# Eleven weight casts and five casts of h on GpSimd in the first sixteen steps of an attention and MLP kernel

## Chip, cores and metric

The kernel runs on one core of one Trainium2 chip. The metric is device time in microseconds (us) of one execution, the lower the better. Engines: PE is TensorE (PEld its weight loads), DVE is VectorE, ACT is ScalarE, POOL is GpSimd, SP is SyncE, which issues most transfers.

## The reference, cut to what matters

```python
def _attn_ref(q, k, v):                       # (8, 8, 576, 64) each, window of 128
    scores = scale * q @ k.T + bias           # bias = -slope(head) * distance
    scores = where(0 <= distance < 128, scores, -1e9)
    attn = exp(scores - max(scores)); attn = attn / (sum(attn) + 1e-9)
    return attn @ v

x = attention output as (4608, 512)
h = maximum(x @ w_in, 0.0)                    # w_in (512, 2048)
out = (h * h) @ w_out                         # w_out (2048, 512)
```

All numbers are float32.

## The kernel before, in words

The 4608 tokens are cut into `NCH` = 9 chunks `c` of 512 tokens. For each chunk the attention output `x` is built for `NP` = 4 pairs of heads `p`, and the two products with the weights run over `NF` = 16 steps `f`, each with 128 of the 2048 middle columns. To keep float32 accuracy on TensorE, each operand is split into a high half (a cast to fp32r) and a low half (what the cast left), and each product is made of three: high by high, high by low, low by high. So `gemm1(c, f)` is 12 products of 128x128 by 128x512 into the one bank `g` (line 194), and `gemm2(c, f)` is 12 products into four banks `acc` (line 223).

Weights come in once, as pairs of 32-bit words in `raw[f]` (two transfers of 512 KB a step, line 159), and `convert(f)` turns them in five instructions of 128x1024: a Prelu on ScalarE (line 165), a shift on VectorE (167), a shift with an or on VectorE (169), the cast of the high half `wh` (171) and the subtraction on VectorE that gives the low half `wl` (173). In the planner these are `("c", f, 0)` to `("c", f, 4)`. The cast is on GpSimd for f in `CASTS`, on ScalarE otherwise.

Between the two products of a step stand four instructions of 128x512, `("h1", f, 0)` to `("h1", f, 3)`: the relu out of bank `g` on ScalarE (204), the square (for chunk 0 on ScalarE at line 209, on VectorE at line 207 for f in `SQUARES`), the cast `hh` on ScalarE (211) and the subtraction `hl` on VectorE (213).

Attention for chunk 0 is done in eight wide segments `k` = 0 to 7 (two a pair of heads), with steps named by letters: `s` scores (TensorE, line 508), `u` the largest score (VectorE, 518), `e` exp (ScalarE, 525), `r` the sum's reciprocal (VectorE, 258 and 259), `n` the normalisation (GpSimd at line 537, VectorE at 535 for k in `NORMS`), `z` transposes (TensorE, 544 and 547), `o` and `m` copies out of their banks (`o` at line 277 on ScalarE, on VectorE for k in `COPIES`; `m` at 551 on VectorE), `x` the values (TensorE, 291, into the bank that the planner calls `xa`), `h` the cast of the high half (ScalarE, 301) and `l` the subtraction for the low half (VectorE, 304), which frees `xa`. Chunks from 1 on are done in couples `q` from 4 on: scores (392), copies on ScalarE (419, 426, the planner's `base`), folds on VectorE (438, 442), then the same softmax in segments (244, 251, 258, 262), a transpose on VectorE (313), a way through DRAM (317, 322), two selects on GpSimd (326) and the values (338).

Everything up to the end of chunk 0's sixteen steps is put in order by `start(K)`. It adds steps to a `Plan` with an engine, a cost in us, the steps that must come before, a due time and the buffers taken and given back; `NUDGE` shifts single due times. `Plan.run` then goes through a list schedule: of the steps that can begin within 0.1 us (or `WAIT` times a step's cost) of the earliest, on its engine, the one due first is issued. What comes out is the order of instructions on each engine (PE, DVE, Activation, Pool, SP); on the chip each engine follows its own order and waits for semaphores. `Plan.shares` tells which steps of GpSimd and VectorE the planner keeps apart in time. A weight's steps may begin after the steps that `HOLD(f)` names: `('n', 3)` is the normalisation of segment 3, `('z', 7)` the transposes of segment 7.

The order that TensorE follows in the chunk's start: `g1a` (the first nine products of `gemm1(0, 0)`, after `("x", 7)` and `("l", 0)` to `("l", 5)`), the rest of it, `gemm1(0, 1)`, `gemm1(0, 2)`, `gemm2(0, 0)`, `gemm1(0, 3)`, and so on in turns, with scores and values of the couples in between. From chunk 1 on a plain loop gives the order on TensorE, and a scheduler orders the other engines.

Of the kernel before, what the change touches and what calls it, by code (L numbers as in the profile page):

```python
# [25 lines left out]
NSEG = 2 * NP * NCH  # L26
PER = S // 64
HEAT = 16
HOLD = lambda f: (('n', 3),) if f < 1 else (('n', 6),) if f < 2 else (('z', 7),)
WAIT = 0.1  # L30
HAND = {"SP": 2.0, "PE": 0.25}
PORT = ('t', 'c', 'h1')
CONVERT = (('Activation', 1.2), ('DVE', 0.7), ('DVE', 1.2), ('Activation', 1.15), ('DVE', 1.2))
# [3 lines left out]
SOON = (("z", 7),)  # L37
FIRST = 39
APART = lambda i, f, b: i == 0 and f % 4 == 0 and b < 2
CASTS = (0, 2, 15,)  # L40
COPIES = (3,)
SQUARES = (6,)
NORMS = (7,)
NUDGE = {
# [6 lines left out]
}  # L51
SYNC = mybir.DependencyInfo(mybir.DependencyClass.Sync, mybir.DependencyReason.DATA)
ORDER = mybir.DependencyInfo(mybir.DependencyClass.NoSync, mybir.DependencyReason.DATA)
# [8 lines left out]
class Kern:  # L62
# [98 lines left out]
    def convert(self, f):  # L161
# [8 lines left out]
        yield  # L170
        (nc.gpsimd.tensor_copy if f in CASTS else nc.scalar.copy)(wh, flo)
        yield
# [13 lines left out]
    def gemm1(self, c, f):  # L186
        nc = self.nc
        xs = [self.x[c, p] for p in range(NP)]
        g = self.g1.tile([128, 512], F32, name="g")
        i = 0  # L190
        for cc in range(NCC):
            wl, wh = self.block(0, f, cc)
            for w, part in ((wh, 0), (wh, 1), (wl, 0)):
                nc.tensor.matmul(g, w, xs[cc][:, part], start=i == 0, stop=i == 11)  # L194
                i += 1
                if (c, f, i) == (0, 0, 9):
                    yield
        yield
        r = self.hp.tile([128, 512], F32, name="r", bufs=1)
        hh = self.hp.tile([128, 512], F32R, name="hh")  # L200
        hl = self.hp.tile([128, 512], F32R, name="hl")
        self.h[c, f] = hh, hl
        with self.tc.high_priority(offset=100):
            self.relu = nc.scalar.activation(r, g, AF.Relu)  # L204
        yield
        if c or f in SQUARES:
            nc.vector.tensor_tensor(r, r, r, op=ALU.mult)  # L207
        else:
            nc.scalar.activation(r, r, AF.Square)
        yield  # L210
        nc.scalar.copy(hh, r)  # L211
        yield
        nc.vector.tensor_tensor(hl, r, hh.bitcast(F32), op=ALU.subtract)  # L213

# [18 lines left out]
class Segment:  # L233
# [42 lines left out]
    def out(self):  # L276
        (self.nc.vector.tensor_copy if self.k in COPIES else self.nc.scalar.copy)(self.own, self.z)

# [209 lines left out]
class Wide(Segment):  # L488
# [40 lines left out]
    def norm(self):  # L529
        for i in (0, 1) if self.skip else (None,):  # L530
            m, a = (slice(None), 0) if i is None else (slice(i, 4, 2), self.first[i])
            t, rec = self.t[:, m, a:256], self.nm[:, 8:12][:, m]
            if self.k in NORMS:
                for j in range(t.shape[1]):
# [23 lines left out]
class Plan:  # L558
# [7 lines left out]
        self.steps[name] = (engine, us, after, due + NUDGE.get(name, 0), do, rooms(take), rooms(free))  # L566

    def shares(self, name):
        return self.steps[name][0] == "Pool" or (name[0] in PORT and self.steps[name][0] == "DVE")

    def room(self, name, n):
        self.count[name] = [0.0] * n
# [1 line left out]
    def run(self):  # L574
        left, end, clock = dict(self.steps), {}, {"SP": 0.8}
        while left:
# [16 lines left out]
            on, span = self.steps[first[2]][:2]  # L593
            same = [r for r in ready if self.steps[r[2]][0] == on and r[0] <= first[0] + max(0.1, WAIT * span)]
            t, due, name = min(same, key=lambda r: (r[1], r[0]))
# [13 lines left out]
def start(K):  # L609
    P = Plan()  # L610
    for name, n in (("sc", 1), ("sa", 1), ("xa", 1), ("at", 1), ("zp", 1), ("tw", 4), ("t", 3), ("pp", 2), ("ld", 3), ("g", 1)):
        P.room(name, n)
    do = lambda fn, *a: lambda: fn(*a)
# [27 lines left out]
    for k in range(8):  # L641
        G = Wide(K, k)
        c, p, sg = G.c, G.p, G.sg
        n = lambda s, *m: (s, k, *m)
        after = [("q", c, p, 0), ("q", c, p, 1)][: sg + 1] + ([("s", k - 1)] if k else [])
        chain = lambda s: ((s, k - 1),) if k else ()
        d, slot, w = 4.0 * k, "sa" if k % 2 else "sc", 0.75 if G.skip else 1.0
        P.add(n("s"), "PE", 0.9 * w, tuple(after), d, G.scores, slot)
        for m in range(4):
            P.add(n("u", m), "DVE", 0.35 * w, (n("u", m - 1) if m else n("s"), ("k", p)), d - 1.5, do(G.top, m), None if m else "tw", slot if m == 3 else None)  # L650
            P.add(n("e", m), "Activation", 0.48 * w, (n("u", m),) + ((n("e", m - 1),) if m else ()), d + 0.5, do(G.exp, m))
        P.add(n("r"), "DVE", 0.4, (n("e", 3),), d + 1, G.sums)
        P.add(n("n"), *(("DVE", 0.9 * w) if k in NORMS else ("Pool", 2.05 * w)), (n("r"),), d + 1, G.norm)
        P.add(n("z"), "PE", 0.9 * w, (n("n"),) + chain("z"), d - 3, G.turn, ("at", "zp", "pp"), "tw")
        P.add(n("o"), "DVE" if k in COPIES else "Activation", 0.6, (n("z"),), d - 2, G.out, None, "at")
        P.add(n("m"), "DVE", 0.62 if w == 1 else 0.36, (n("z"),), d + 1, G.also, None, "zp")
        P.add(n("x"), "PE", 1.0, (n("m"), n("o"), ("v", c, p)) + chain("x"), d + 4, G.values, "xa", "pp")
        P.add(n("h"), "Activation", 0.4, (n("x"),), d + 2, G.high)
        P.add(n("l"), "DVE", 0.36, (n("h"),), d + 2, G.low, None, "xa")
        if sg == 1:  # L660
            P.add(n("ld"), "free", 0.0, (n("x"),), d + 2, None, None, None if p == 3 else "ld")
    for q in range(4, 9):
# [7 lines left out]
        for s in (1, 0):  # L670
            G, k = C.both[s], 2 * q + s
            n = lambda s, *m: (s, k, *m)
# [18 lines left out]
    for f in range(NF):  # L691
        d, last = CONV(f), ("w", f)
        g = K.convert(f)
        for i, (engine, us) in enumerate(CONVERT):
            if i == 3 and f in CASTS:
                engine, us = "Pool", 1.5
            P.add(("c", f, i), engine, us, (last,) + HOLD(f), d, lambda g=g: next(g, None))
            last = ("c", f, i)

    last = ["wide", ("x", 7)] + [("l", k) for k in range(6)]  # L700
    for f in range(NF + 2):
        if f < NF:
            g = K.gemm1(0, f)
            step, n = lambda g=g: next(g, None), len(CONVERT) - 1
            if f == 0:
                P.add("g1a", "PE", 2.1, tuple(last) + (("c", f, n),), GO, step, "g")
                last = ["g1a", ("l", 6), ("l", 7)]
            P.add(("g1", f), "PE", 2.8 if f else 0.7, tuple(last) + (("c", f, n),), 500 if f else GO, step, "g" if f else None)
            for i, (engine, us) in enumerate((("Activation", 0.6), ("Activation", 0.65), ("Activation", 0.62), ("DVE", 0.78))):
                if i == 1 and f in SQUARES:  # L710
                    engine, us = "DVE", 0.75
                free = "g" if i == 0 else None
                P.add(("h1", f, i), engine, us, (("h1", f, i - 1) if i else ("g1", f),), -1, lambda g=g: next(g, None), None, free)
            last = [("g1", f)]
        if 1 < f < NF:
            P.add(("g2", f - 2), "PE", 2.8, (("g1", f), ("h1", f - 2, 3)), 500, do(K.gemm2, 0, f - 2))
            last.append(("g2", f - 2))
# [4 lines left out]
def tile_attn_moe(ctx: ExitStack, tc: tile.TileContext, *aps):  # L722
    K = Kern(ctx, tc, *aps)
    K.const()
    with tc.manual_schedule(engines={ENGINES["PE"]}):
        with tc.manual_schedule(engines={e for n, e in ENGINES.items() if n != "PE"}):
            start(K)
# [86 lines left out]
```

## Time and profile before

| what | us |
|---|---|
| median of 3 runs | 956.03 |
| lowest and highest | 955.96, 956.26 |
| the profiled execution's own time | 956.69 |
| its span, first to last instruction | 955.0 |
| TensorE matmul busy in the span | 946.8 (99%) |
| VectorE, ScalarE, GpSimd busy | 496.5, 417.6, 214.6 |

The span is what the trace covers; the rest of the execution's own time lies around it. A busy share over the whole span says little here, since the start and the long loop behind it have different limits: the start is read in stretches and in the order of time on each engine. A row of a timeline has the start, the duration, the engine, the line of the kernel, the operation, the tile written and the tile read with their shapes, and in brackets the idle time of the engine ahead of it with what ended that. Rows that follow each other with the same line are merged (x12). TensorE's granted clock was 1.00 in the whole span, its level of 2.4 GHz.

### The profile page before, as it was taken

To read this page: it belongs to the slowest core of one execution; us is meant where nothing else is said; L and a number is where in the kernel's file an instruction comes from. 1 tells how busy PE (TensorE), PEld (TensorE's weight loads), DVE (VectorE), ACT (ScalarE), POOL (GpSimd) and SP (SyncE) were. 2 spreads that over 40 slices of the span, in tenths; PEclk is the share of its full clock that TensorE was granted. 3 is DMA by queue.
4 is the path that set the end of the run, shared out by engine and by line. 5 is a ranking of instruction groups with operands and counts; after the bars stand their busy time and mean duration, and the time that the engine had idled before them with its cause. 6 is when DMAs were issued, how large, how long until landed. Compare 5 with 4: busy or idle time off the path is not lost.

```text
span 955.0 us, 17236 instructions
## 1 busy us (share of the span) xinstructions
PE 946.8 (99%) x6392; PEld 796.4 (83%) x6392; DVE 496.5 (52%) x1334; ACT 417.6 (44%) x1107; POOL 214.6 (22%) x254
## 2 busy tenths in 40 slices
PE   9899999999999999999999999999999999999998
PEld 5688888888888888888888888888888888888886
DVE  6998864445545455444544454455545444433222
ACT  7898743333444444434433343334344343332222
POOL 4123331222222222222222222221222212220000
PEclk9999999999999999999999999999999999999999
DMA  9974423322433333222433232333322231111001
GB/s 349 404 274 151 146 67 119 83 64 68 124 84 83 84 88 107 72 77 73 127 84 83 77 108 71 83 83 96 114 74 71 71 95 45 45 45 45 1 1 44
DMA packets 72883, 95.10 MB, mean 100 GB/s; under 512 B 8032, under 2 KB 41952, under 8 KB 72800
## 3 DMA queue, kind: packets, MB, share of 16 engines
q1 hardware_dynamic: 72368, 93.36, 32.9%
q8 instruction: 50, 0.82, 0.4%
q10 hardware_dynamic: 432, 0.66, 0.2%
q14 instruction: 33, 0.27, 0.1%
HBM read 67.76 MB, written 26.21 MB: 98 GB/s over the span
## 4 chain that ended last, share of the span: by engine, by line
PE 95%; DMA 4%; ACT 0%; issue 0%; DVE 0%; SPq 0%; DVEq 0%
PE acc L223 42%; PE g L194 42%; PE at L338 6%; PE s L392 3%; PE g L392 2%; DMA raw<-in_dram 2%; DMA wide<-in_dram 1%; DMA qk<-in_dram 1%; PE at L392 0%; ACT raw L165 0%; DVE raw L167 0%; ACT t L426 0%; ACT t L419 0%; ACT o L229 0%; DVE xu L304 0%
## 5 line engine op out<-in xcount | busy, mean ns | idle before, releaser
L194 PE MATMUL g<-xu,w 128*128 128x512 f32 x1728 | 423.3, 394 | 0.8 <-issue 0.8
L194 PEld LDWEIGHTS g<-xu,w 128*128 128x128 f32 x1728 | 344.1, 209 | 56.2 <-issue 1.5
L223 PE MATMUL acc<-hh,w 128*128 128x512 f32 x1152 | 386.2, 396 | 0.0
L223 PEld LDWEIGHTS acc<-hh,w 128*128 128x128 f32 x1152 | 223.9, 194 | 44.3 <-issue 0.7
L207 DVE TENSOR_TENSOR r<-r 128x512 f32<-128x512 f32 x129 | 103.0, 799 | 248.2 <-ACT r L204 246.9
L204 ACT ACTIVATE r<-g 128x512 f32<-128x512 f32 x144 | 85.9, 596 | 326.8 <-PE g L194 316.4
L223 PE MATMUL acc<-hl,w 128*128 128x512 f32 x576 | 226.8, 394 | 0.0
L326 POOL TENSOR_SCALAR_AFFINE_SELECT pp<-pp 128x512 f32<-128x512 f32 x128 | 107.1, 840 | 211.1 <-DMA pp<-way 162.2
L213 DVE TENSOR_TENSOR hl<-r,hh 128x512 fp32r<-128x512 f32 x144 | 108.6, 754 | 69.3 <-ACT hh L211 68.4
L262 POOL TENSOR_TENSOR t<-t,nm 128x512 f32<-128x512 f32 x64 | 82.0, 1281 | 263.9 <-DVE nm L259 145.9
L223 PEld LDWEIGHTS acc<-hl,w 128*128 128x128 f32 x576 | 112.0, 194 | 19.9
L251 ACT ACTIVATE t<-t,nm 128x128 f32<-128x128 f32 x256 | 100.1, 393 | 56.8 <-DVE nm L244 56.8
L211 ACT CAST hh<-r 128x512 fp32r<-128x512 f32 x144 | 89.1, 619 | 75.8 <-DVE r L207 74.2
L438 DVE COPY_PREDICATED t<-cst,s 64x256 f32<-64x256 int32 x100 | 44.5, 445 | 41.0 <-ACT t L426 22.4
L313 DVE STREAM_TRANSPOSE pp<-t 128x512 f32<-128x512 f32 x64 | 45.2, 707 | 38.0 <-POOL t L262 37.9
L338 PEld LDWEIGHTS at<-pp,v 128*64 128x64 f32 x1024 | 55.2, 137 | 11.2 <-issue 10.8
L338 PE MATMUL at<-pp,v 128*64 128x128 f32 x1024 | 63.0, 276 | 0.0
L244 DVE CUSTOM_DVE_ANT_0 t<-t,cst 128x128 f32<-128x128 f32 x256 | 59.0, 293 | 1.0
L251 ACT ACTIVATION_READ_ACCUMULATOR t<-t,nm 128x1 f32 x256 | 48.3, 189 | 0.0
L392 PE MATMUL s<-qk 64*64 64x64 f32 (+2 forms) x1168 | 47.5, 251 | 0.8 <-ACT raw L165 0.8
L392 PEld LDWEIGHTS s<-qk 64*64 64x64 f32 x1168 | 43.0, 133 | 1.0 <-ACT raw L165 1.0
L428 POOL MEMSET t<- 64x128 f32 (+1 forms) x44 | 10.0, 228 | 138.7 <-PE g L392 129.8
(63 smaller groups left out, 472.6 us busy)
## 6 DMA issues: line engine op xcount, KB each, us to landing
raw<-in_dram SPq DMA_DIRECT2D x32, 512.0 KB, 8.7
way<-pp SPq DMA_DIRECT2D x256, 64.0 KB, 1.8
pp<-way SPq DMA_DIRECT2D x64, 256.0 KB, 2.8
qk<-in_dram SPq DMA_DIRECT2D x32, 320.0 KB, 3.6
v<-in_dram SPq DMA_DIRECT2D x32, 320.0 KB, 3.0
qk<-in_dram SPq DMA_DIRECT2D x38, 256.0 KB, 4.2
out_dram<-o SPq DMA_DIRECT2D x35, 256.0 KB, 4.3
v<-in_dram SPq DMA_DIRECT2D x3, 256.0 KB, 4.9
```

The source lines that it names most:

```text
L194: nc.tensor.matmul(g, w, xs[cc][:, part], start=i == 0, stop=i == 11)
L204: self.relu = nc.scalar.activation(r, g, AF.Relu)
L207: nc.vector.tensor_tensor(r, r, r, op=ALU.mult)
L211: nc.scalar.copy(hh, r)
L213: nc.vector.tensor_tensor(hl, r, hh.bitcast(F32), op=ALU.subtract)
L223: nc.tensor.matmul(self.acc[m], w, h, start=(f == 0 and i == 0), stop=(f == NF - 1 and i == 2))
L244: self.nc.vector.tensor_tensor_reduce(self.t[:, m], self.t[:, m], self.K.nrel(2 * self.p + m // 2), -0.125, BIG, ALU.add, ALU.min, self.nm ...
L251: return self.nc.scalar.activation(self.t[:, m], self.t[:, m], AF.Exp, bias=nm[:, m : m + 1], scale=-1.0, accum_out=nm[:, 4 + m : 5 + m],)
L262: self.nc.gpsimd.tensor_tensor(self.t, self.t, self.nm[:, 8:12].unsqueeze(2).to_broadcast([128, 4, 128]), op=ALU.mult)
L326: nc.gpsimd.affine_select(to, self.own, pattern=[[-32 * sign, 4], [0, 4], [-sign, 32]], compare_op=op, fill=0.0, base=0, channel_multiplie ...
L338: self.nc.tensor.matmul(self.X[r, o : o + 128].rearrange("p (a c) -> p a c", a=4), v[:, 2 * sg + k, r], src[:, :, 2 * j + i], start=sg == ...
L392: mm = nc.tensor.matmul(to, qk[r, q0 : q0 + 64], qk[r, k0 : k0 + 64 * n], start=True, stop=True, skip_group_check=True,)
```

## The change

The high halves of eleven weights instead of three are cast on GpSimd (`CASTS`), and of `hh` those of f = 1, 4, 8, 9 and 13 in chunk 0 (`SPLITS`, new). One square more goes to VectorE (f = 4 and 8 instead of 6), the normalisation of segment 0 goes to VectorE beside that of segment 7, and the copies `o` of segments 2 and 4 instead of 3. The planner's costs of `e`, `o`, `h` and of GpSimd's cast are others, `HOLD` names segment steps one earlier for f from 1 on, `WAIT` is 0, `NUDGE` is another list, and `Plan.shares` returns False: GpSimd and VectorE are planned side by side.

```diff
-HOLD = lambda f: (('n', 3),) if f < 1 else (('n', 6),) if f < 2 else (('z', 7),)
-WAIT = 0.1
+HOLD = lambda f: (('n', 3),) if f < 1 else (('n', 5),) if f < 2 else (('z', 6),)
+WAIT = 0
@@
-CASTS = (0, 2, 15,)
-COPIES = (3,)
-SQUARES = (6,)
-NORMS = (7,)
+CASTS = (0, 1, 2, 3, 4, 7, 10, 12, 13, 14, 15,)
+COPIES = (2, 4,)
+SPLITS = (1, 4, 8, 9, 13,)
+SQUARES = (4, 8,)
+NORMS = (0, 7,)
 NUDGE = {
-    ('u', 1, 3): -17, ('r', 2): 96, ('r', 4): -63, ('l', 4): -29, ('u', 5, 3): 104.5, ('r', 5): -13.5,
...
+    ('w', 4): 194, ('w', 7): 41.5, ('m', 0): 8.5, ('o', 2): -4.5, ('u', 3, 3): 81.5, ('u', 4, 3): 181,
+    ('u', 5, 3): -382, ('u', 6, 0): -20, ('e', 6, 0): -60, ('t', 9, 1): 1.5, ('square', 8): 20, ('t', 11, 3): 11,
+    ('c', 0, 2): 4, ('c', 0, 4): 8, ('c', 6, 1): 1.5, ('c', 10, 1): 8.5,
 }
@@
-        nc.scalar.copy(hh, r)
+        (nc.gpsimd.tensor_copy if c == 0 and f in SPLITS else nc.scalar.copy)(hh, r)
@@
     def shares(self, name):
-        return self.steps[name][0] == "Pool" or (name[0] in PORT and self.steps[name][0] == "DVE")
+        return False
@@
-            P.add(n("e", m), "Activation", 0.48 * w, (n("u", m),) + ((n("e", m - 1),) if m else ()), d + 0.5, do(G.exp, m))
+            P.add(n("e", m), "Activation", 0.49 if w == 1 else 0.44, (n("u", m),) + ((n("e", m - 1),) if m else ()), d + 0.5, do(G.exp, m))
@@
-        P.add(n("o"), "DVE" if k in COPIES else "Activation", 0.6, (n("z"),), d - 2, G.out, None, "at")
+        P.add(n("o"), *(("DVE", 0.61) if k in COPIES else ("Activation", 0.48)), (n("z"),), d - 2, G.out, None, "at")
@@
-        P.add(n("h"), "Activation", 0.4, (n("x"),), d + 2, G.high)
+        P.add(n("h"), "Activation", 0.3, (n("x"),), d + 2, G.high)
@@
             if i == 3 and f in CASTS:
-                engine, us = "Pool", 1.5
+                engine, us = "Pool", 1.25
@@
+                if i == 2 and f in SPLITS:
+                    engine, us = "Pool", 0.7
```

## Rows read from the trace of the kernel before

**Rows 1.** Stretches: window, us, busy PE, PEld, DVE, ACT, POOL, clock, DMA, GB/s
```profile
7.00:37.20 30.20, 28.84 (x298) 19.05 (x294) 28.14 (x107) 26.52 (x83) 13.66 (x14) 1.00 1.04 399
37.20:49.70 12.50, 10.89 (x91) 8.81 (x89) 11.77 (x32) 11.49 (x29) 1.10 (x1) 1.00 1.03 406
49.70:70.00 20.30, 20.30 (x116) 17.13 (x115) 19.85 (x44) 19.67 (x33) 4.86 (x6) 1.00 0.73 268
37.20:130.80 93.60, 91.99 (x642) 76.83 (x641) 84.89 (x178) 75.47 (x161) 26.68 (x32) 1.00 0.60 203
```
**Rows 2.** Timeline of TensorE, 37 to 53 us: first products and gaps
```profile
37.22 3.18 PE L194 MATMUL g<-xu,w 128*128 128x512 f32 x12
...
41.57 0.34 PE L392 MATMUL s<-qk 64*64 64x192 f32 x1 [0.81 <-ACT raw L165]
...
42.93 3.09 PE L194 MATMUL g<-xu,w 128*128 128x512 f32 x12
46.82 3.04 PE L194 MATMUL g<-xu,w 128*128 128x512 f32 x12 [0.80 <-issue]
...
52.50 2.96 PE L194 MATMUL g<-xu,w 128*128 128x512 f32 x12
```
**Rows 3.** Timeline of VectorE, 29 to 51 us
```profile
29.07 1.09 DVE L258 TENSOR_SCALAR nm<-nm 128x4 f32<-128x4 f32 x1
...
30.41 1.14 DVE L535 TENSOR_SCALAR tw<-tw,nm 128x256 f32<-128x256 f32 x4
...
31.80 1.22 DVE L173 TENSOR_TENSOR w<-raw,w 128x1024 fp32r<-128x1024 f32 x1
32.93 0.42 DVE L304 TENSOR_TENSOR xu<-acc,xu 128x256 fp32r<-128x256 f32 x1
33.26 0.68 DVE L551 COPY pp<-acc 128x512 f32<-128x512 f32 x1
...
35.73 0.42 DVE L304 TENSOR_TENSOR xu<-acc,xu 128x256 fp32r<-128x256 f32 x1
...
39.41 1.36 DVE L438 COPY_PREDICATED t<-cst,s 64x256 f32<-64x256 int32 x3 [0.60 <-ACT t L426]
...
41.45 2.36 DVE L173 TENSOR_TENSOR w<-raw,w 128x1024 fp32r<-128x1024 f32 x2
...
49.04 0.69 DVE L213 TENSOR_TENSOR hl<-r,hh 128x512 fp32r<-128x512 f32 x1
49.65 1.22 DVE L173 TENSOR_TENSOR w<-raw,w 128x1024 fp32r<-128x1024 f32 x1
```
**Rows 4.** Timeline of ScalarE, 30 to 38 us
```profile
30.36 0.37 ACT L301 CAST xu<-acc 128x256 fp32r<-128x256 f32 x1 [0.48 <-PE acc L291]
...
34.33 0.37 ACT L301 CAST xu<-acc 128x256 fp32r<-128x256 f32 x1 [0.67 <-PE acc L291]
...
35.90 1.21 ACT L171 CAST w<-raw 128x1024 fp32r<-128x1024 f32 x1
...
37.61 0.60 ACT L419 COPY t<-at 128x512 f32<-128x512 f32 x1
```
**Rows 5.** Timeline of GpSimd: a cast, and the longest wait for a transfer
```profile
28.95 1.19 POOL L171 CAST w<-raw 128x1024 fp32r<-128x1024 f32 x1 [2.75 <-ACT tw L525]
...
72.43 1.52 POOL L326 TENSOR_SCALAR_AFFINE_SELECT pp<-pp 128x512 f32<-128x512 f32 x2 [8.27 <-DMA pp<-way]
```
**Rows 6.** Instructions grouped by line and shape, 37.2 to 130.8 us
```profile
L173 DVE TENSOR_TENSOR w<-raw,w 128x1024 fp32r<-128x1024 f32 x15 | 19.4, 1304 | 0.1
L171 ACT CAST w<-raw 128x1024 fp32r<-128x1024 f32 x12 | 13.6, 1143 | 3.4 <-DVE raw L169 3.4
L213 DVE TENSOR_TENSOR hl<-r,hh 128x512 fp32r<-128x512 f32 x15 | 11.9, 795 | 2.7 <-ACT hh L211 2.5
L211 ACT CAST hh<-r 128x512 fp32r<-128x512 f32 x15 | 9.3, 623 | 0.4
L171 POOL CAST w<-raw 128x1024 fp32r<-128x1024 f32 x2 | 2.2, 1104 | 6.6 <-DVE raw L169 3.4 <-ACT t L419 3.2
```

5 rows, old and new, of the table NUDGE are left out of this document.

## The prediction

> **What bounds the kernel now.** I read the busy times by stretch first, to find the stretch in which the end of the run is still open [rows 1]. TensorE (the first busy column) is full from 49.7 us on: it works 20.30 of 20.30 us up to 70 us, and between 37.2 and 130.8 us it works 91.99 of 93.60 us, while the part up to 49.7 us alone holds 10.89 of 12.50. So all of the 1.61 us that TensorE lacks between its first large product and the sixteenth lies ahead of 49.7 us. From there on the time is a fixed row of products; it ends earlier only if that row begins earlier or the gaps ahead of 49.7 us close, and later only if a new gap opens.
>
> Next I read TensorE's order of time around the gaps [rows 2]. The first large product (`g1`, step f=0) starts at 37.22 us. A gap of 0.81 us lies before 41.57, where the scores of couple 5 wait; the product of f=1 then starts at 42.93. Another gap of 0.80 us lies before the product of f=2 at 46.82, which has to wait until its bank `g` has been read. By 52.50 us, f=3, there are no gaps any more.
>
> Then I read what the other engines do just ahead of these starts. Between 7 and 37.2 us VectorE is busy 28.14 of 30.20 us and ScalarE 26.52; from 37.2 to 49.7 us 11.77 and 11.49 of 12.50; from 49.7 to 70 us 19.85 and 19.67 of 20.30. GpSimd has 13.66, 1.10 and 4.86 in the same three [rows 1]. So the start is a queue on VectorE and ScalarE, with GpSimd nearly free from 28 to 50 us, and this is what the change draws on. VectorE is the scarcer of the two.
>
> **The path to the first large product.** It stands behind the values of segment 7 in TensorE's order, and those behind `l` of segment 6, which frees the one bank `xa`. On VectorE I count three delays on that way [rows 3 to 5]. First, the sum `r` of segment 7 (line 258, four columns) begins at 29.07 us and ends at 30.16, just behind the end of GpSimd's cast of weight 0 (28.95 + 1.19 = 30.14): it has waited the cast out, and of its 1.09 us I count 0.9 as delay, an estimate that leaves 0.2 for its own work. Second, `l` of segment 5 starts at 32.93 although ScalarE had cast its `h` by 30.36 + 0.37; the last of what stands ahead of it is the subtraction for weight 0, 31.80 to 32.93: 1.13 us. Third, `l` of segment 6 starts at 35.73, although its `h` was ready at 34.33 + 0.37 = 34.70: 1.03 us behind integer work for weight 1. Together 3.1 us, all of it order.
>
> **The change part by part.** All of it is in `start`; the loop behind it isn't touched, and no transfer is added or taken away, though SP's list can be put out in another order.
>
> *Casts.* Eleven instead of three go to GpSimd, so eight more: at 1.10 us each [rows 6] 8.8 us more there, and 8 x 1.14 = 9.1 us less on ScalarE. *Blocks of h.* Five casts of 128x512 leave ScalarE, 5 x 0.62 = 3.1 us [rows 6]. The trace doesn't show that cast on GpSimd: half a 128x1024 cast is 0.55 us, a whole one 1.10; I take 0.62, since the tile has half the columns, and so 3.1 us. GpSimd gets 11.9 us more in all, in the 93.6 us in which it is busy for 26.68 [rows 1]: it has room. In its queue a cast can stand behind a select that awaits a transfer; the longest such wait is 8.27 us [rows 5]. What waits for the cast is the subtraction on VectorE and all behind that in VectorE's list.
>
> *Cast of weight 1.* It stands on ScalarE at 35.90 us for 1.21, ahead of the copies of couple 4's scores (37.61) [rows 4]. From these follow the folds on VectorE at 39.41, and behind the folds, in VectorE's list, the subtraction for weight 1 at 41.45 [rows 3], for which the product of f=1 waits until 42.93; the folds also free the bank that the scores of couple 5 go into, at 41.57 [rows 2]. (The row there names ScalarE's weight work as what came last; the folds, done when the subtraction starts at 41.45, lie as close, and it is their bank, so I follow them.) With that cast on GpSimd the copies can start up to 37.61 - 35.90 = 1.7 us earlier. Bounds 0 and -1.7; I take -0.9, a little over the gap of 0.81 us, since the values of segment 7, whose cast `h` comes in between, don't move with it.
>
> *Order around segments 5 to 7.* Weight 1 may now be turned from norm 5 on (norm 6 before), the others from the transposes of segment 6 on (7 before), and the planner's costs for `o`, `h` and `e` differ. The three delays above can go, or others can take their place: weight 0 stays with GpSimd and weight 1 joins it. Bounds -3.1 and +1.5 (the next point); I take half of the gain, -1.5.
>
> *Norm 0 and the copies `o`.* Norm 0 goes to VectorE, at most the 1.14 us that norm 7 takes there; of `o`, segments 2 and 4 go to VectorE and 3 leaves it, which adds one copy of about 0.68 [rows 3]. That is up to 1.8 us more on an engine with 2.1 us idle in that stretch, against a shorter way for segment 0. I take 0 and keep +1.5 (1.8 less the 0.3 us by which it idles early on anyway, an estimate) as the other end of the point above. *Squares.* Two instead of one on VectorE (+0.69 us, the undisturbed time of line 213, also 128x512): nothing on the path.
>
> *GpSimd beside VectorE.* The planner no longer keeps them apart, so more operations of VectorE will be held up as the sum at 29.07 was. Two kinds show what that costs now: line 173 takes 1.304 us in the mean and line 213 0.795 [rows 6], against 1.22 and 0.69 in single instructions with no GpSimd work beside them [rows 3]. Times 15 each this is 1.3 + 1.6 = 2.9 us, beside 26.68 us of GpSimd: 0.11 us for each. These two are 31.3 of VectorE's 84.89 us; for the others I double the rate, 0.2, an estimate. The added 11.9 us would so cost VectorE 1.3 to 2.4 us; the other end is that each of them holds it up, 11.9 us. I take 3, near the measured rate, with a little more because nothing plans around it. VectorE idles 93.60 - 84.89 = 8.7 us between 37.2 and 130.8 us, which covers this; where the cover fails it costs TensorE directly (second rival). I put it at 0 on the path, bounds 0 and +4.
>
> *What is late next.* The gap of 0.80 us before f=2 [rows 2] waits for the read of bank `g` behind product f=1, with no other product to put in between: it stays.
>
> Sum: -0.9 - 1.5 = -2.4 us. The profiled execution took 956.69 us, its span 955.0; the median of the runs is 956.03, 0.66 below the profiled one. I take the change off the median: 953.6.
>
> The Trainium skill, SBUF — State Buffer, section "Who interferes with whom", has a rule against this change: a VectorE instruction in a two-port mode, or with two inputs in SBUF, and a GpSimd instruction that reads SBUF exclude each other for the whole instruction, and the later one waits in full. The sum at 29.07, which ends within 0.02 us of GpSimd's cast, agrees with it. By that rule alone no overlap is free, and the sum goes towards the second rival.
>
> **The rivals.** *First: the start is no shorter, 955.9 (954.2 to 957.5).* VectorE carries the start and gets no lighter; ScalarE's relief only moves the waits. For it: VectorE idles only 0.73 us in the 12.5 us before 49.7, and norm 0 and one copy are added to it ahead of that. Against it: two of the three delays are pure order, and the wait at 41.57 leads back to a ScalarE cast that goes. This also holds the case in which the new lists come out nearly as the old ones.
>
> *Second: GpSimd holds VectorE up until TensorE runs dry, 959.0 (958 to 961).* The place is 49.7 to 70 us, where VectorE idles 0.45 us and ScalarE 0.63. The weight for f=3 is ready at 49.65 + 1.22 = 50.87 us and its product starts at 52.50 [rows 2, 3], a margin of 1.63 us. If the casts of weights 3, 4 and 7 and the blocks h of 1 and 4 come in here, GpSimd has 3 x 1.10 + 2 x 0.62 = 4.5 us more. Where over 0.45 + 1.63 = 2.1 us of it holds VectorE up, TensorE waits: 2.4 us at the most here, and by the same working a like amount once more where weights 10 to 14 are cast, less what VectorE can idle away there. I price it at 3 us and more than the gain at the start being lost: 959.0. For it: the overlap seen at 29.07 is complete. Against it: 0.2 us per us of GpSimd gives 0.9 us here, below the 2.1. A cast behind a select that waits up to 8.27 us for its transfer [rows 5] would end in the same place, by another way.
>
> **How the numbers follow.** A gain at the start that holds: 0.47; no net gain: 0.31; TensorE starved: 0.22. The measurement can tell about 0.2%, 1.9 us, from no change, so under 954.1 is faster and over 957.9 slower. The forecast is 953.6, and its own range goes from 951.2 (both terms at their ends, -1.7 and -3.1) to 954.1. For 8 in 10 the range must hold the first rival and much of the second. The lower end is 951.0, which is those ends and 0.2 us of the second gap; the upper end is 959.5. Faster 0.47, same 0.31, slower 0.22.
>
> **What would show it.** Right: the first large product at about 35.7 us instead of 37.22; product f=1 some 4.8 us behind it instead of 5.7; product f=3 near 50.1; TensorE full from about 47.3 us on. ScalarE should be some 12 us lighter between 37.2 and 130.8 us, GpSimd 12 us heavier, and VectorE 2 to 5 us heavier in the same work, all in longer instructions, of lines 173 and 213 among others. Wrong: a first product at 37 us or later; a gap on TensorE behind 50 us, with a subtraction of a weight (line 173) just ended in front of it; waits on GpSimd of lines 171 or 211 behind a select.

## The result and the profile after

The changed kernel takes 960.91 us (960.84 to 961.25) against 956.05 us for the kernel before, a ratio of 1.0051 with a 95% interval of 1.0040 to 1.0062: 4.9 us slower, where 2.4 us faster was forecast (medians of six runs each). The profiled execution took 960.86 us, its span 959.1.

The stretches of after answer to [rows 1]; columns: window, us, then busy us of PE, PEld, DVE, ACT and POOL, the granted clock, DMA share and GB/s.

```profile
7.00:37.20 30.20, 28.97 (x296) 20.50 (x298) 28.20 (x108) 26.39 (x85) 13.51 (x13) 1.00 1.04 399
37.20:49.70 12.50, 11.25 (x94) 9.01 (x94) 11.77 (x31) 10.52 (x24) 4.49 (x4) 1.00 1.03 406
49.70:70.00 20.30, 19.79 (x151) 16.05 (x150) 20.10 (x38) 15.01 (x32) 9.30 (x10) 1.00 0.71 238
37.20:130.80 93.60, 88.04 (x616) 71.70 (x616) 90.38 (x173) 60.10 (x140) 44.26 (x41) 1.00 0.57 195
```

Up to 49.7 us TensorE works a little more than before. Behind that, where it had been full, it now lacks time: 88.04 instead of 91.99 of the 93.6 us. ScalarE is 15.4 us lighter (12 forecast), VectorE 5.5 heavier, and GpSimd 17.6 heavier, though only some 12 us of work came to it. The stretch is fixed in time, and by its end TensorE has done less (616 against 642 instructions), so a comparison over the same work follows with the first experiment.

TensorE in the order of time (answers to [rows 2]) shows where:

```profile
35.39 3.63 PE L192 MATMUL g<-xu,w 128*128 128x512 f32 x12
...
40.19 3.06 PE L192 MATMUL g<-xu,w 128*128 128x512 f32 x12 [1.17 <-issue]
...
50.38 0.63 PE L192 MATMUL g<-xu,w 128*128 128x512 f32 x2
...
51.32 2.61 PE L192 MATMUL g<-xu,w 128*128 128x512 f32 x10 [0.31 <-DVE w L171]
...
57.39 2.73 PE L192 MATMUL g<-xu,w 128*128 128x512 f32 x10 [0.20 <-DVE w L171]
...
87.81 0.37 PE L390 MATMUL s<-qk 64*64 64x192 f32 x1 [0.77 <-DVE t L440]
...
100.39 0.74 PE L192 MATMUL g<-xu,w 128*128 128x512 f32 x2 [0.52 <-POOL w L169]
...
102.49 2.62 PE L192 MATMUL g<-xu,w 128*128 128x512 f32 x10 [1.36 <-DVE w L171]
...
115.04 0.37 PE L390 MATMUL s<-qk 64*64 64x192 f32 x1 [1.16 <-DVE t L440]
```

The first product starts at 35.39 us instead of 37.22 and that of f=3 at 50.38 instead of 52.50: the start is shorter. In the start one gap is left, 1.17 us ahead of f=1: ScalarE's relu out of bank `g` ends just before it, at 39.50 + 0.60 = 40.10 us, and the scores of couple 5, which stood there before, now come behind f=1. Then the product of f=3 stops after two of its twelve parts for the subtraction of its weight, and so does f=4. At 100.39 the product of f=10 waits for GpSimd's cast of its weight and again for the subtraction behind it; two sets of scores wait for folds on VectorE. The starts of products in the traces, in us:

| kernel | f=0 | f=1 | f=3 | f=8 | f=10 | f=11 | f=12 | chunk 1, f=0 |
|---|---|---|---|---|---|---|---|---|
| before | 37.22 | 42.93 | 52.50 | 84.07 | 98.91 | 104.51 | 111.69 | 138.54 |
| after | 35.39 | 40.19 | 50.38 | 83.48 | 100.39 | 107.75 | 116.51 | 143.42 |
| after, less before | -1.83 | -2.74 | -2.12 | -0.59 | +1.48 | +3.24 | +4.82 | +4.88 |

The whole difference is there when chunk 1 begins. All that was gained, and 4.8 us more, goes between f=3 and f=12: 1.5 us of it up to f=8, 5.4 from there on. The gaps in this stretch add up to 4.3 of these 6.9 us; the rest lies in rows that count as busy, 61.81 us from f=3 to f=12 for the same products that took 59.19 us before.

What holds the weight of f=10 up, first GpSimd in the order of time (answers to [rows 5]):

```profile
91.16 1.62 POOL L324 TENSOR_SCALAR_AFFINE_SELECT pp<-pp 128x512 f32<-128x512 f32 x1 [5.01 <-DVE nm L257]
92.73 0.61 POOL L209 CAST hh<-r 128x512 fp32r<-128x512 f32 x1
...
98.30 2.03 POOL L169 CAST w<-raw 128x1024 fp32r<-128x1024 f32 x1 [1.15 <-DVE raw L167]
100.26 1.11 POOL L209 CAST hh<-r 128x512 fp32r<-128x512 f32 x1
```

and VectorE in the same microseconds (answers to [rows 3]):

```profile
93.38 1.17 DVE L211 TENSOR_TENSOR hl<-r,hh 128x512 fp32r<-128x512 f32 x1 [1.18 <-POOL hh L209]
...
98.16 1.22 DVE L171 TENSOR_TENSOR w<-raw,w 128x1024 fp32r<-128x1024 f32 x1
99.30 1.60 DVE L165 TENSOR_SCALAR raw<-raw 128x1024 int32<-128x1024 int32 x1
100.81 1.63 DVE L171 TENSOR_TENSOR w<-raw,w 128x1024 fp32r<-128x1024 f32 x1
```

GpSimd's cast takes 2.03 us instead of 1.10, and the shift and the subtraction of VectorE beside it 1.60 and 1.63 us, where the same sizes take 0.69 and 1.22 undisturbed. The ends fit waiting in turn: the cast ends 0.95 us behind the subtraction that began at 98.16 us, the shift 0.57 us behind the cast, and the subtraction of f=10 1.07 us behind GpSimd's next cast, each a little less than its undisturbed 1.10, 0.69 and 1.22 us. Earlier in the same list VectorE sits idle for 1.18 us, up to 93.38, for GpSimd's cast of the block h of f=8; that cast takes 0.61 us, but it stands behind a select of 1.62 us. The groups from 37.2 to 130.8 us say the same of the whole stretch (answers to [rows 6]; behind the bar busy us and mean ns of one):

```profile
L171 DVE TENSOR_TENSOR w<-raw,w 128x1024 fp32r<-128x1024 f32 x15 | 20.7, 1388 | 0.3 <-POOL w L169 0.3
...
L167 DVE SCALAR_TENSOR_TENSOR raw<-raw 128x1024 int32<-128x1024 int32 x14 | 20.3, 1447 | 0.3
...
L169 POOL CAST w<-raw 128x1024 fp32r<-128x1024 f32 x9 | 13.6, 1516 | 17.0 <-DVE raw L167 12.9 <-ACT raw L163 4.1
...
L211 DVE TENSOR_TENSOR hl<-r,hh 128x512 fp32r<-128x512 f32 x13 | 12.6, 973 | 1.7 <-POOL hh L209 1.7
...
L209 POOL CAST hh<-r 128x512 fp32r<-128x512 f32 x5 | 4.7, 932 | 7.0 <-ACT r L207 6.2 <-DVE r L205 0.7
```

### The profile page after: what moved, and what is told of

It reads as the page before. It is cut to its first block, busy times and chain, and to the rows that moved or that the text cites. A ratio compares the mean times of both kernels' runs of the same rounds, so it can differ in the third digit from the quotient of the medians.

```text
span 959.1 us, 17238 instructions
## 1 busy us (share of the span) xinstructions
PE 947.1 (99%) x6389; PEld 796.4 (83%) x6392; DVE 508.4 (53%) x1340; ACT 404.6 (42%) x1092; POOL 233.7 (24%) x265
## 4 chain that ended last, share of the span: by engine, by line
PE 92%; DVE 5%; issue 1%; DMA 1%; POOL 0%; SPq 0%; ACT 0%; DVEq 0%; POOLq 0%
PE acc L221 40%; PE g L192 39%; PE at L336 6%; PE s L390 2%; PE g L390 2%; DVE w L171 1%; DMA raw<-in_dram 1%; PE g L119 1%; DVE hl L211 1%; DVE raw L165 1%; PE acc L289 1%; DVE raw L167 0%; DVE t L242 0%; PE s L506 0%; DVE pp L311 0%
## 5 line engine op out<-in xcount | busy, mean ns | idle before, releaser
L205 DVE TENSOR_TENSOR r<-r 128x512 f32<-128x512 f32 x130 | 106.6, 820 | 247.9 <-ACT r L202 246.3
L211 DVE TENSOR_TENSOR hl<-r,hh 128x512 fp32r<-128x512 f32 x144 | 112.3, 780 | 66.9 <-ACT hh L209 65.0
L260 POOL TENSOR_TENSOR t<-t,nm 128x512 f32<-128x512 f32 x64 | 84.3, 1318 | 248.8 <-DVE nm L257 139.4
L209 ACT CAST hh<-r 128x512 fp32r<-128x512 f32 x139 | 86.0, 619 | 77.1 <-DVE r L205 75.5
```

What stands on the lines that cost most here:

```text
L209: (nc.gpsimd.tensor_copy if c == 0 and f in SPLITS else nc.scalar.copy)(hh, r)
L260: self.nc.gpsimd.tensor_tensor(self.t, self.t, self.nm[:, 8:12].unsqueeze(2).to_broadcast([128, 4, 128]), op=ALU.mult)
```

## The experiments

### Taking GpSimd's new work back, with the lists kept

A step's engine can be changed where it is issued, without the planner knowing. TensorE's and VectorE's lists then stay as they are, instruction for instruction.

```diff
-        (nc.gpsimd.tensor_copy if f in CASTS else nc.scalar.copy)(wh, flo)
+        (nc.gpsimd.tensor_copy if f in (0, 2, 15) else nc.scalar.copy)(wh, flo)
-        (nc.gpsimd.tensor_copy if c == 0 and f in SPLITS else nc.scalar.copy)(hh, r)
+        nc.scalar.copy(hh, r)
```

> The changed kernel with every list kept as it is, TensorE's and VectorE's instruction for instruction; only the eight casts of weights and the five casts of h that the change gave to GpSimd are issued on ScalarE at the same places. Theory (GpSimd's added work holds VectorE up, by overlap and by its own lateness): VectorE loses the 6 us of longer instructions that it has more than before, TensorE's gaps behind 50 us close for the most part, 954 to 957 us. Rival (the other list of VectorE and TensorE is bad by itself): the gaps stay, 960 to 962 us.

Measured 956.75 us (ratio to before 1.0007, 0.9998 to 1.0017): 4.16 us of the 4.86 lost come back. The stretch in this run:

```profile
37.20:130.80 93.60, 91.68 (x636) 75.36 (x636) 88.63 (x194) 73.55 (x170) 28.07 (x31) 1.00 0.61 203
```

and the three kinds of VectorE's instructions in it, grouped by line and shape:

```profile
L171 DVE TENSOR_TENSOR w<-raw,w 128x1024 fp32r<-128x1024 f32 x15 | 19.0, 1271 | 0.4 <-ACT w L169 0.3
...
L167 DVE SCALAR_TENSOR_TENSOR raw<-raw 128x1024 int32<-128x1024 int32 x14 | 19.2, 1369 | 0.3
...
L211 DVE TENSOR_TENSOR hl<-r,hh 128x512 fp32r<-128x512 f32 x14 | 11.3, 808 | 0.6 <-ACT hh L209 0.5
```

With the same list, a subtraction of line 171 is 117 ns shorter than in after, line 167 78 ns, line 211 165 ns: times 15, 14 and 13 that is 1.8 + 1.1 + 2.1 = 5.0 us of VectorE in this stretch. TensorE has 91.68 us again. Over the same work, from the start to the first product of chunk 1, before, after and this run are:

```profile
0.00:138.54 138.54, 134.11 (x1012) 104.58 (x1013) 118.05 (x304) 108.66 (x264) 42.93 (x52) 1.00 0.68 238
0.00:143.42 143.42, 135.16 (x1009) 104.78 (x1013) 127.34 (x313) 95.64 (x249) 63.16 (x64) 1.00 0.66 230
0.00:139.13 139.13, 134.34 (x1009) 104.72 (x1013) 121.46 (x313) 106.88 (x262) 44.81 (x51) 1.00 0.68 237
```

So the 11.9 us of work on GpSimd cost VectorE 127.34 - 121.46 = 5.9 us, 0.49 us for each, and took GpSimd itself 63.16 - 44.81 = 18.4 us. Another 3.4 us on VectorE (121.46 less 118.05) come with the changed lists and VectorE's added norm, copy and square.

Each half alone, the first with only the second line of the diff, the other with only the first:

> As the first, but only the five casts of h go back to ScalarE; the eight weight casts stay on GpSimd. By the theory the price goes with GpSimd's time: 3.1 of 11.9 us go, so a quarter of what the first run gives back, 959 to 960 us. Rival (a late cast of h, 1.46 us long once, is what delays the subtractions): most of the gain comes here, 956 to 957.

Measured 959.43 us (1.0036, 1.0023 to 1.0049): 1.5 us come back.

> As the first, but only the eight casts of weights go back to ScalarE; the casts of h stay on GpSimd. By the theory three quarters of the first run's gain, 955 to 958 us; by the rival that blames the casts of h, 960 to 961.

Measured 957.80 us (1.0019, 1.0010 to 1.0028): 3.1 us come back. The two make 4.6 us, near the 4.16 of both; three quarters of GpSimd's time give two thirds to three quarters of the gain. The blocks of h are no special case.

### Giving the same work to GpSimd in the lists of before

```diff
-        (nc.gpsimd.tensor_copy if f in CASTS else nc.scalar.copy)(wh, flo)
+        (nc.gpsimd.tensor_copy if f in (0, 1, 2, 3, 4, 7, 10, 12, 13, 14, 15) else nc.scalar.copy)(wh, flo)
-        nc.scalar.copy(hh, r)
+        (nc.gpsimd.tensor_copy if c == 0 and f in (1, 4, 8, 9, 13) else nc.scalar.copy)(hh, r)
```

> The kernel before with its own lists; only the engine of the eight casts and the five casts of h is GpSimd, at the places where ScalarE had them. Theory: VectorE is held up by some us more and TensorE gets gaps, 958 to 962 us. Rival (the list alone costs the time, GpSimd's casts are free): 955 to 957 us.

Measured 959.11 us (1.0033, 1.0021 to 1.0044), 3.1 us slower. So the work costs 3 to 4 us in either list, and the other list is not what makes it dear: by itself it costs at most the 0.7 us that the first run lies above before, which the runs can't tell from nothing.

### Work that nobody waits for

The first run's kernel, with copies of 128x512 from a constant into a spare tile at the places of the thirteen casts:

```diff
+        self.spare = self.c.tile([128, 512], F32, name="spare")
...
+        if f in CASTS and f not in (0, 2, 15):
+            for _ in range(2):
+                nc.gpsimd.tensor_copy(self.spare, self.cst[:, 256:768])
...
+        if c == 0 and f in SPLITS:
+            nc.gpsimd.tensor_copy(self.spare, self.cst[:, 256:768])
```

> The kernel of the first run (after's lists, all the casts in question on ScalarE), with GpSimd work added that nobody waits for, at the places of the thirteen casts: for a weight two copies of 128x512 from a constant into a spare tile, for a block of h one, 21 in all, some 12 us. (One buffer of the output tiles is given up for the spare tile.) Theory (overlap alone holds VectorE up, 0.5 us for each us of GpSimd): VectorE's instructions between 37 and 131 us grow by 4 to 7 us and the time goes to 959 to 961 us. Rival (the casts cost because VectorE waits for their results): VectorE grows by under 3 us, 956 to 958.

Measured 963.16 us (1.0072, 1.0057 to 1.0087), 6.4 us more than the first run, more than expected: the 21 copies took GpSimd nearer to 20 than to 12 us. And with `nc.gpsimd.memset(self.spare, 0.0)` in place of each copy:

> As the run with spare copies, but the 21 operations are memsets of 128x512, which read nothing. If what GpSimd and VectorE exclude each other from is the reading of SBUF, VectorE's instructions with two inputs don't grow, and the time stays near the first run's, 956 to 957.5 us. If any GpSimd instruction holds VectorE up, it is as slow as the spare copies, 958.5 to 961. Each also shows whether the buffer given up costs anything.

Measured 957.46 us (1.0015, 1.0006 to 1.0025). The groups of the run with copies from 37.2 to 130.8 us, GpSimd's new work at the places of the weights and the subtraction of the weights (line 175 here):

```profile
L173 POOL COPY spare<-cst 128x512 f32<-128x512 f32 x14 | 13.7, 976 | 0.6
...
L175 DVE TENSOR_TENSOR w<-raw,w 128x1024 fp32r<-128x1024 f32 x15 | 22.2, 1485 | 0.0
```

and the same groups of the run with memsets:

```profile
L173 POOL MEMSET spare<- 128x512 f32 x14 | 8.3, 596 | 0.5
...
L175 DVE TENSOR_TENSOR w<-raw,w 128x1024 fp32r<-128x1024 f32 x15 | 19.0, 1270 | 0.4 <-ACT w L170 0.3
```

The stretch as a whole, with copies:

```profile
37.20:130.80 93.60, 88.33 (x616) 71.62 (x616) 91.28 (x171) 70.06 (x151) 48.01 (x48) 1.00 0.57 194
```

and with memsets:

```profile
37.20:130.80 93.60, 91.86 (x636) 75.27 (x636) 89.62 (x194) 72.45 (x164) 37.91 (x49) 1.00 0.60 201
```

The memsets leave the subtraction at 1.270 us, as in the first run (1.271); the copies make it 1.485, and TensorE falls to 88.33 us, near the 88.04 of after, where with memsets it keeps 91.86. Nobody reads the spare tile, so no late result of the copies themselves can cost anything; what differs between the two runs is that the copies read SBUF and take longer. So it is the reading of SBUF by GpSimd, at the same time as VectorE, that costs: 963.16 - 957.46 = 5.7 us. The 0.7 us by which the memset run lies above the first run are hardly clear of the noise. In the traces of both runs TensorE has a gap ahead of f=15 that the first run hasn't, 1.10 us with copies and 0.89 with memsets; whether it comes from a longer queue on GpSimd or from the buffer given up is not shown. In the changed kernel the late casts come on top (0.52 us of waiting at f=10); how the price divides between the two was not measured. The conflict of readers is the rule of the Trainium skill that the prediction cites, SBUF — State Buffer, section "Who interferes with whom"; the same section says that a GpSimd instruction that only writes SBUF doesn't hold up a VectorE instruction with two SBUF inputs, and the memset run agrees (1.270 against 1.271 us).

### VectorE's other additions

```diff
-        if c or f in SQUARES:
+        if c or f == 6:
-        (self.nc.vector.tensor_copy if self.k in COPIES else self.nc.scalar.copy)(self.own, self.z)
+        (self.nc.vector.tensor_copy if self.k == 3 else self.nc.scalar.copy)(self.own, self.z)
-            if self.k in NORMS:
+            if self.k == 7:
```

> The kernel of the first run with VectorE's other additions undone in the same lists: norm 0 is issued on GpSimd, the copies o of segments 2 and 4 on ScalarE and that of 3 on VectorE, the squares of f = 4 and 8 on ScalarE and that of 6 on VectorE. VectorE has some 2.5 us less. Theory (VectorE's load sets when weights 3 and 4 are ready, and the earlier start runs into it): 1 to 2 us faster than the first run, 954.7 to 955.8 us. Rival (ScalarE, full until 37 us, takes back what VectorE gives; or order alone counts): 956.3 to 958.

Measured 957.62 us (1.0015, 1.0006 to 1.0025): 0.9 us slower, so the theory's time did not come and the rival's did. TensorE in the order of time, the first product of this run:

```profile
37.40 3.21 PE L192 MATMUL g<-xu,w 128*128 128x512 f32 x12
```

and that of the first run:

```profile
36.27 3.20 PE L192 MATMUL g<-xu,w 128*128 128x512 f32 x12
```

It lost 1.13 us there and won nothing behind it. It tests the theory only in part: most of what VectorE lost lies ahead of 37.2 us (25.88 instead of 27.98 us busy from 7 us on). From f=3 to f=12 VectorE has 59.19 instead of 60.10 us, and the stretch is no shorter (61.92 against 61.81 us). To see whether norm 0 or the copies bring the start forward by themselves, the lists of before had them issued as after has them:

```diff
-            if self.k in NORMS:
+            if self.k in (0, 7):
```

> The kernel before with one thing changed in its lists: norm 0 is issued on VectorE, as after has it, at the place where GpSimd had it. If norm 0 there is what brings the first product forward by about 1.1 us (the run that took norm 0 and the copies back had it 1.13 us later), the first product starts near 36.1 us; since product f=1 and its weight don't move with it, the time falls by 0 to 1 us, 955.0 to 956.0. Rival (VectorE, full in the start, loses the 1.0 us that the norm takes): first product after 37.5 us, 956.5 to 957.5.

Measured 956.14 us (1.0000, 0.9991 to 1.0009), first product at 37.18 us: nothing changes, neither of the two came true. With the copies as well:

```diff
-        (self.nc.vector.tensor_copy if self.k in COPIES else self.nc.scalar.copy)(self.own, self.z)
+        (self.nc.vector.tensor_copy if self.k in (2, 4) else self.nc.scalar.copy)(self.own, self.z)
```

> As the run with norm 0 on VectorE in the lists of before, with the copies o of segments 2 and 4 also on VectorE and that of 3 on ScalarE, as after has them. If the copies are what counts, the first product is earlier here than in that run and the time 0.5 us or more below it; if they cost VectorE what they give ScalarE, it is within 0.3 us of it.

Measured 957.41 us (1.0014, 1.0005 to 1.0022), first product at 38.61: 1.3 us slower than with norm 0 alone, outside both expectations. In the lists of after these parts and the squares are worth 1.1 us at the first product; in the lists of before norm 0 and the copies cost 1.4 there. Neither is a gain in the lists of before, so what they are worth depends on the lists around them; the squares were not tried alone.

### The planner's rule that keeps the two engines apart

```diff
     def shares(self, name):
-        return False
+        return self.steps[name][0] == "Pool" or (name[0] in PORT and self.steps[name][0] == "DVE")
```

> The changed kernel with the planner again keeping GpSimd apart from VectorE's steps of weights, h and folded scores (the former body of shares); casts, engines and all else as after. The lists come out anew. Theory (overlap is the cause): the plan spreads the overlaps, VectorE's growth falls and the time to 955 to 959 us. Rival (GpSimd's time is too much wherever it lies, or the nudges fit only the other plan): 960 us and more.

Measured 974.13 us (1.0191, 1.0176 to 1.0206). This is the rival's time, and the rival named two causes. The overlaps became fewer: GpSimd's casts and VectorE's subtractions are shorter than in after (1.516 and 1.388 us there), the subtractions not as short as in the first run (1.271). The groups from 37.2 to 130.8 us:

```profile
L169 POOL CAST w<-raw 128x1024 fp32r<-128x1024 f32 x7 | 8.5, 1219 | 24.8 <-DVE raw L167 20.6 <-DMA qk<-in_dram 4.1
...
L171 DVE TENSOR_TENSOR w<-raw,w 128x1024 fp32r<-128x1024 f32 x13 | 17.3, 1334 | 6.7 <-ACT w L169 4.0 <-POOL w L169 2.5
```

But all lists come out anew, and in these TensorE waits long for single weights, in the order of time:

```profile
75.74 5.89 PE L192 MATMUL g<-xu,w 128*128 128x512 f32 x12 [3.47 <-ACT w L169]
...
112.94 1.22 PE L192 MATMUL g<-xu,w 128*128 128x512 f32 x2 [5.41 <-POOL w L169]
```

This says nothing on the price of an overlap: the planner's rule, costs and nudges belong together, and one can't be turned alone.

### Closing the gaps that were left

The first run still has the shorter start (36.27 and 50.41 us for f=0 and f=3), yet at f=11 it is 0.5 us behind before. Four steps that stood in front of a gap were moved in its lists, and the cast of weight 1 given back to GpSimd (in the diff, cut, each step `name` is issued just ahead of the step `before`):

```diff
-        (nc.gpsimd.tensor_copy if f in (0, 2, 15) else nc.scalar.copy)(wh, flo)
+        (nc.gpsimd.tensor_copy if f in (0, 1, 2, 15) else nc.scalar.copy)(wh, flo)
...
+        for name, before in [(('c', 5, 0), ('c', 6, 0)), (('c', 3, 4), ('r', 8)), (('c', 4, 4), ('c', 5, 1)), (('c', 12, 3), ('c', 12, 4))]:
+            ...
```

> The kernel of the first run with the cast of weight 1 on GpSimd again, as after has it, and four steps moved in the lists: on ScalarE the Prelu of weight 5 behind the relu, square and cast of f=0, and the cast of weight 12 behind those of f=10; on VectorE the subtraction of weight 3 ahead of the sum of segment 8, and that of weight 4 ahead of the shift of weight 5. Theory (what is left of the earlier start is lost where weight 3 and the reading of bank g come late): the first product at about 35.4 us, that of f=3 without its gaps, 1.0 to 2.0 us faster than the first run, 954.8 to 955.8 us, below the kernel before. Rival (VectorE's total sets the pace, so what is moved is late elsewhere): within 0.5 us of the first run, 956.2 to 957.2.

Measured 956.71 us (1.0006, 0.9997 to 1.0015), as the first run: the rival. The gap inside f=3 is gone, and others stand elsewhere (TensorE in the order of time, the products of f=2 to f=4):

```profile
45.13 3.06 PE L192 MATMUL g<-xu,w 128*128 128x512 f32 x12 [0.53 <-issue]
...
50.83 2.96 PE L192 MATMUL g<-xu,w 128*128 128x512 f32 x12
...
56.91 1.34 PE L192 MATMUL g<-xu,w 128*128 128x512 f32 x4 [0.33 <-ACT r L202]
```

The first product starts at 35.84 us, not at the 35.4 expected, and f=3 0.4 us later than in the first run. No version tried beats the kernel before.

## Why the prediction was wrong, point by point

**What bounds the kernel** held: nothing changed the row of products behind chunk 0, and the whole difference of the medians, 4.86 us, is the 4.88 by which chunk 1 begins later.

**The gain at the start** had the right size in part by luck. Forecast were -1.5 us for the first product and -2.4 for f=3; measured -1.83 and -2.12. The term of -0.9 us between the two, for the cast of weight 1, came to -0.29, and not by its way: without that cast on ScalarE the copies of couple 4's scores start 1.14 us earlier (36.47 us), but the folds behind them no earlier (39.48 against 39.41), and the first run, with the cast on ScalarE again, reaches f=3 at 50.41 us as well. The gap in front of product f=1 didn't close: it is 1.17 us. The gap before f=2, which was to stay, went, since the scores of couple 5 now stand there. So the 4.8 us from f=0 to f=1, just as forecast, come from the order. The point "norm 0 and the copies" was put at 0 with a loss as its other end; in after's lists these parts and the squares, undone together, were worth 1.1 us at the first product.

**"GpSimd beside VectorE" is the step that failed**, with the words "I put it at 0 on the path, bounds 0 and +4". It costs 4.2 us (first run), a little over that upper end. Three things in it were wrong. The rate: I took 3 us of VectorE for 11.9 us of GpSimd, 0.25 us for each, from rows of a kernel whose planner keeps the two apart; measured over the same work it is 5.9 us, 0.49. GpSimd's own side was not in the sum: its casts went from 1.10 us to 1.516 in the mean, so weights also arrive later. And the cover was added up over 93.6 us (8.7 us of idle VectorE), while TensorE needs each weight at its own time; the margin of 1.63 us at f=3 was used up by the start that came 2.12 us earlier, before any conflict was counted against it: the first run, without the added work, waits 0.48 us in product f=3 too.

**The second rival is what happened**, and by its mechanism, as the spare copies and memsets show. It was given 0.22 and 959.0 us; the measured time is 1.9 us above that, within the rival's own 958 to 961 and 1.4 above the range. Its places were right, but not their shares: behind f=3 and f=4, from 49.7 to 70 us, TensorE lacks only 20.30 - 19.79 = 0.5 us of busy time, where 2.4 us at the most were named first; most goes around f=10, among the weights 10 to 14 that the rival named second, with 0.52 and 1.36 us of waiting in one product, and at the scores at 87.81 and 115.04 us, 0.77 and 1.16, which I hadn't listed among those that wait for VectorE. Its other way, a cast behind a select, is seen once, at f=8: VectorE idles 1.18 us for it, ahead of the work for the weight of f=10. The trace puts the end of that select's own wait down to VectorE, not to a transfer, and what the 1.18 us cost TensorE was not measured by itself.

**The first rival** gives the time that is left, though not its mechanism: with GpSimd's work taken back the start is 2.1 us shorter at f=3, and the end, 956.75 us, is where it was. Why the gain is used up behind f=3 is not settled. Moving the steps in front of the gaps didn't bring it back, which would fit VectorE's total as the bound: from f=3 to f=12 it is busy for 60.10 of 61.81 us in the first run, and for 54.56 of 59.19 before. But the run that took 2.5 us off VectorE, 0.9 of them there, is no shorter from f=3 to f=12, and its start came later.

**The median less the profiled time** (0.66 us) was rightly taken off: from the first product of chunk 1 to the end the profiled execution of before takes 816.43 us and after 815.72, and the run with before's lists and norm 0 moved has 815.72 too. That 0.7 us belongs to the execution, not to the lists.

## What to carry to other kernels

An engine with idle time is not free room if it shares something with the engine that is short of time: ask first what the two exclude each other from. Take the rate of such a conflict from a stretch in which nothing keeps them apart, count it on both engines, and hold it against the margin of each deadline, not against the sum of idle time. Where the order was made by a planner and fitted by hand, parts of the change can't be priced alone; changing only the engine of a step in lists that stay fixed tells the price of the work from that of the order.

## What the runs showed of the hardware that I had not expected

GpSimd's copies and VectorE's instructions slow each other even where GpSimd's own operation is a plain copy with one input: 128x512 took 0.976 us in the mean beside VectorE and a memset of that size 0.596, where in after a cast of 128x512 that ran while VectorE was idle took 0.61 (at 92.73 us). In the run with the planner's rule the granted clock of TensorE was lower after its long waits. Its stretches, the product behind the wait of 3.47 us alone, what follows it, and a stretch ahead of it:

```profile
75.74:81.63 5.89, 5.85 (x13) 4.16 (x14) 4.84 (x14) 4.19 (x16) 1.18 (x2) 0.50 0.31 123
81.63:90.00 8.37, 7.52 (x31) 5.90 (x30) 6.25 (x10) 5.05 (x10) 1.33 (x3) 0.96 0.24 50
62.00:72.00 10.00, 9.97 (x113) 8.09 (x111) 8.81 (x16) 3.82 (x6) 4.58 (x5) 1.00 0.58 177
```

That product ran at 0.50, the lower of the two levels (1.2 of 2.4 GHz), and took 5.89 us where others take about 3.0: the wait cost TensorE nearly twice its length. In after, whose gaps between 37 and 131 us are 1.4 us at the most, the clock stayed at 1.00.
